# Output products of a SwiGLU block: a 15-product scheme on 2x3 blocks in place of 7-product Strassen, one core of a Trainium2

## The chip, the cores and the metric

The kernel runs on one core of one Trainium2 chip. The metric is the time of one execution on the device in microseconds (us); lower is better. The core has a matrix engine (TensorE, "PE" in the profile, its weight loads "PEld"), a vector engine (VectorE, "DVE"), a scalar engine (ScalarE, "ACT"), GpSimd ("POOL") and a queue engine that here only starts DMA transfers (SyncE, "SP"). Each engine runs its own queue of instructions in order and waits for others through semaphores. SBUF is the on-chip memory of 128 partitions; PSUM is the memory into which PE writes, eight banks of 128 partitions by 512 float32 columns.

## The reference

```python
# x: (8, 4096, 192), weight: (8, 7); w_gate, w_val: (192, 1536); w_out: (1536, 192)
w = softmax(weight, axis=-1)                      # one set of 7 taps for each of 8 heads
out[b, s, h*24 + g] = sum_k w[h, k] * x_pad[b, s + k, h*24 + g]     # 6 zero rows ahead
x = out.reshape(32768, 192)
xn = x / sqrt(mean(x * x, axis=-1) + 1e-6) * rms_g
g = xn @ w_gate
silu = g * (1 / (1 + exp(-g)))
return (silu * (xn @ w_val)) @ w_out              # (32768, 192) float32
```

The weights of the second part come in float64 and are turned to float32 at the start of the kernel. All arithmetic is float32.

## The kernel before

The 32768 tokens are cut into 32 pairs of 1024 (PT). A pair is two groups of 512 tokens (T), held with the 192 features over partitions in three chunks of 64 (KP). The 1536 inner features are 12 chunks of 128 (FC), four units of three (NU, NF).

Pair 0 is computed plainly (plain, L1060, and outer, L1101) while the weights are still being converted. Pairs 1 to 31 use fast matrix products, and each has two stages on PE:

- **Inner products (L798).** For each unit, a scheme of 15 products stands for the 18 plain ones (3 chunks of inner features x 3 chunks of the input x 2 groups). The upper 64 partitions hold the same for the value weights, so each product is two matmuls of 64 rows, which run side by side: half 0 for the gate, half 1 for the value. That is 60 products, 120 matmuls. Between products, ACT and DVE copy, fork and add PSUM banks (Unit.do: S a copy to SBUF, F a bank copied into another, D, C, N and R sums of a bank and a saved tile). G is the SiLU on ACT; M multiplies SiLU and value to a tile of ht, on POOL or DVE (L850).
- **Output products (L938).** The product of the gated tiles with w_out is a Strassen product: 7 products, each over six blocks of 128 inner features (k), in three PSUM banks X, Y and Z. Operands are sums of tiles of the two groups (Pair.sum, L970 and L968: early, nt, more and tls hold them) and differences of blocks of w_out (out_sums, L864, made once in the array x0's place). PE takes them as four column groups of 32 output columns: for a block, two matmuls of 384 token columns on column groups 0 and 1, two of 256 and then two of 128 on groups 2 and 3. Afterwards DVE transposes the results in blocks of 32x32 (turn, L953) and SP stores them (st0, st1, L1024).

Meanwhile the input of a later pair is prepared: DVE does the seven taps in PSUM banks of its own (part_tap, L476, words cv in the order below), ACT the squares (L492), DVE a sum over features, POOL the factor and the scaling (L509, L512, L530); the result goes through DRAM (place) and comes back with tokens along the free axis (fetch_part, tiles xb). Eleven sums of these chunks (XSUM, x_sum, L709 on DVE or POOL; L705 and L706 as a copy and an accumulating DMA) are the other operands of the inner products (xc).

An accumulating DMA (letter Q) is issued from POOL's queue: POOL spends an instruction on it and the addition is done by the transfer, without POOL's arithmetic.

**What sets the order.** ORDER is a list of words, gone through once for each pair. "p2" lets the generator of matmuls (Pair.products) emit two steps. Every other word starts with the engine, V (DVE), A (ACT), G (POOL), Q (accumulating DMA from POOL) or D (DMA queue of SP), and then names a step: "AF0.1.2" is fork 0, half 1, unit 2, on ACT; "GS3.0" is the sum of form 3, block 0, on POOL; "VX3" is entry 3 of XSUM on DVE. A minus at the end means that the step belongs to the pair before. Each engine gets its instructions in the order of its own words; what waits for what is derived from the data. Banks come from two lists of four (free; half 0 and half 1), and a matmul that needs a bank waits for the step that gave it back. In a pair there are 120 steps for inner products, then 84 for output products.

Of the kernel before, what the change touches and what calls it, by code (L numbers as in the profile page):

```python
# [19 lines left out]
def kernel(  # L20
# [68 lines left out]
    SPAN = 1509  # L89
    ORDER = (  # L90
        "p2 GX4- VT11- p2 AS40.0.0 GX9- AS40.1.0 p2 AF0.1.0 AF0.0.0 p2 VC.0.0 Dload- p2",
        "VC.1.0 AS41.0.0 VS41.1.0 p2 AS00.1.0 VS00.0.0 p2 Vbc- VD5.0.0 Gmul- p2 VD5.1.0",
        "AS42.0.0 VS42.1.0 AS51.1.0 p2 AS51.0.0 VR1.0.0 p2 VR1.1.0 VR0.0.0 p2 AF2.0.0 VN.1.0",
        "AG0.0.0 p2 VR0.1.0 AF3.0.0 Dplace- AF3.1.0 p2 GM0.1.0 VR2.0.0 p2 VR2.1.0 AS44.1.0",
        "AS44.0.0 VR5.1.0 p2 AG2.0.0 VR3.0.0 p2 GM2.1.0 AS40.0.1 VR3.1.0 AS40.1.1 p2 VR5.0.0",
        "AG4.0.0 p2 VM4.1.0 AF0.0.1 AG5.0.0 VF0.1.1 p2 AG1.0.0 VS41.0.1 GM5.1.0 p1 AS41.1.1",
        "p1 VC.0.1 AG3.0.0 p1 VC.1.1 p1 GM3.1.0 VS00.0.1 p2 AS42.0.1 VS42.1.1 AS00.1.1 GS3.0",
        "p2 VD5.0.1 p1 VD5.1.1 p1 AS51.0.1 QS1.0 VR1.0.1 AS51.1.1 p2 VR1.1.1 AF2.0.1 GS3.1 p2",
        "AF2.1.1 VR0.0.1 AG1.0.1 p1 VR0.1.1 p1 GM1.1.1 VF3.0.1 AF3.1.1 p2 AG0.0.1 VR2.0.1 p1",
        "VR2.1.1 p1 GM0.1.1 AS44.0.1 AS44.1.1 VR5.0.1 p2 GS2.0 VR5.1.1 p2 AS40.0.2 VR3.1.1",  # L100
        "AS40.1.2 p1 VR3.0.1 GM1.1.0 p1 AG4.0.1 AG3.0.1 p1 VM4.1.1 p1 GM3.1.1 VF0.0.2 AF0.1.2",
        "p2 AS41.0.2 VS41.1.2 p1 AG5.0.1 p1 VC.0.2 GM5.1.1 p1 VC.1.2 p1 AS00.0.2 AS00.1.2 p2",
        "QS1.1 AS42.1.2 AS42.0.2 p2 VD5.0.2 GS3.2 p1 VD5.1.2 p1 AS51.0.2 VR1.0.2 AS51.1.2 p2",
        "GS2.1 VR1.1.2 AF2.0.2 p2 AF2.1.2 VR0.0.2 GS1.2 AG1.0.2 p1 VR0.1.2 p1 AG0.0.2 VF3.0.2",
        "GM1.1.2 p1 AF3.1.2 p1 VR2.0.2 AG2.0.1 p1 VR2.1.2 p1 AS44.0.2 GM2.1.1 AS44.1.2 p2",
        "VR3.0.2 AG2.0.2 GS2.2 p1 VR3.1.2 p1 AS40.0.3 VR5.0.2 AS40.1.3 p2 GM2.1.2 AG4.0.2",
        "VR5.1.2 AG3.0.2 p1 VM4.1.2 p1 AF0.0.3 GM0.1.2 p2 AF0.1.3 VS41.0.3 AS41.1.3 p2",
        "GM3.1.2 AG5.0.2 VC.0.3 p1 VC.1.3 p1 AS00.1.3 GS3.3 AS00.0.3 p2 VS42.0.3 AS42.1.3 p2",
        "GS1.3 VD5.0.3 p1 VD5.1.3 p1 AS51.0.3 GM5.1.2 VR1.0.3 AS51.1.3 p2 VR1.1.3 AF2.0.3 p2",
        "GS2.3 AF2.1.3 VR0.0.3 AG1.0.3 p1 VR0.1.3 p1 GS4.2 VF3.0.3 AF3.1.3 p2 AS44.0.3",  # L110
        "VS44.1.3 p1 GM1.1.3 p1 VR5.1.3 p1 VR5.0.3 p1 Acv0_1 VR3.0.3 AG5.0.3 p1 Vcv1_1 Acv0_2",
        "GM5.1.3 p2 VR3.1.3 AG0.0.3 p2 AG3.0.3 Vcv1_2 DfetA GS3.4 p1 AG4.0.3 p1 VR2.0.3 p2",
        "Acv0_0 Vcv2_2 GM3.1.3 p2 VM4.1.3 p2 Vcv2_1 Ac1 GS3.5 p1 AG2.0.3 p1 Vcv3_1 p2 GS1.4",
        "Vcv3_2 p2 Vcv1_0 p2 GS2.4 p1 Vcv2_0 p2 Vcv4_1 p1 As7 GS1.5 DfetB Dst0- p1 VR2.1.3 p2",
        "Vcv5_1 p1 GM0.1.3 p1 Vcv3_0 p2 Vcv6_1 p1 GS2.5 p1 Vcv4_0 p2 Vcv4_2 GS4.0 p2 Vcv5_0",
        "p2 GS4.1 p1 Vcv6_0 p2 Vcv5_2 Ac2 p1 QX0 p1 Vcv6_2 p2 VM2.1.3 Asq p2 GS4.4 p4 VX3 p1",
        "GS4.3 p4 VX6 p1 QX2 p2 VC22 p2 VX1 p2 GS4.5 VT22 p2 Vred p2 QX8 p3 QX7 p2 VC21 p2",
        "VT21 Gpow p2 VX5 p2 VX10 p2 VT12 p1 Dst1 p1",
# [12 lines left out]
    x0 = cst.tile([P, NJ + HALO, D], F32, name="x0")  # L131
# [328 lines left out]
    def part_tap(p, k, j):  # L460
# [306 lines left out]
    class Unit:  # L767
# [87 lines left out]
    woq = wo_sb[:].rearrange("p (k two) d -> p k two d", two=2)  # L855
    woq = woq.rearrange("p k two (m n e) -> p k two m n e", n=2, e=Q)
    B11, B12, B21, B22 = (woq[:, :, i // 2, :, i % 2, :] for i in range(4))
    NM = D // (2 * Q)
    T1, T2, T3, T4 = (tw[:, i].rearrange("p k (m e) -> p k m e", e=Q) for i in range(4))

    def out_sums():
        for dst, a, b in ((T1, B12, B11), (T2, B22, T1), (T3, B22, B12), (T4, B21, T2)):
            for m in range(NM):
                nc.gpsimd.tensor_tensor(  # L864
                    out=dst[:, :, m], in0=a[:, :, m], in1=b[:, :, m], op=ALU.subtract
                )
                yield
# [450 lines left out]
```

## Time and profile before

| what | value |
|---|---|
| median of 3 runs | 2594.16 us (2594.11 to 2594.45) |
| span of the profiled execution, first to last instruction | 2591.7 us |
| the time up to the first inner product of pair 1 | 125.8 us |
| one pair from 1078.22 us on: inner products, output products | 51.92 us, 27.44 us |
| TensorE clock granted | 1.00 |

"Span" leaves out what lies around the first and last instruction. "Busy" counts time in which an engine executes an instruction. Matmuls overlap: float32 matmuls appear twice in the records, and four column groups work at once, so a mean duration of a matmul is not its cost; the time from one stage's start to the next's is. The same holds more weakly on DVE, where the next instruction starts some 0.08 us ahead of the end of the one before: 512 columns take 0.68 as one instruction and 0.60 from start to start. The last matmul of the run ends at 2586.7 us.

### The profile page before, as it was taken

The numbers are of one execution on the slowest core, as the hardware profiler recorded it, in microseconds if no ns is written. First come the engines' busy times: TensorE is split into PE (matmuls) and PEld (weight loads), VectorE is DVE, ScalarE is ACT, GpSimd is POOL, SyncE is SP. The second block draws the span as 40 slices with busy tenths as digits, with TensorE's granted clock in tenths as the row PEclk, the third lists the DMA queues.
The fourth block names the chain that finished last, engine by engine and source line by source line (L and its number), as shares of the span: only waits on it lengthen the run. The fifth ranks groups of instructions, "written<-read, shape, count | busy, mean of one in ns | idle before, by whom it ended". The sixth has DMA issues, their size and how long they took to land.

```text
span 2591.7 us, 61274 instructions
## 1 busy us (share of the span) xinstructions
PE 2580.3 (100%) x23872; PEld 1777.6 (69%) x23872; DVE 2273.3 (88%) x3681; ACT 1554.2 (60%) x2825; POOL 2078.6 (80%) x1791
## 2 busy tenths in 40 slices
PE   9999999999999999999999999999999999999999
PEld 6876666767667666676666676666766666766666
DVE  8899989888889988889889889898988898898975
ACT  6566555675555765556755557655567555676554
POOL 4887788887778877788877888778888788887777
PEclk9999999999999999999999999999999999999999
DMA  6243554334553335443345433354433455334431
GB/s 145 57 83 59 100 100 87 75 65 90 100 100 77 72 68 104 99 83 77 65 91 100 98 76 69 74 104 96 86 76 66 92 100 94 72 72 80 91 76 22
DMA packets 555887, 216.54 MB, mean 84 GB/s; under 512 B 488782, under 2 KB 491342, under 8 KB 555598
## 3 DMA queue, kind: packets, MB, share of 16 engines
q1 hardware_dynamic: 525644, 164.00, 30.7%
q0 software_dynamic: 26208, 47.72, 10.9%
q8 instruction: 187, 3.06, 0.5%
q10 hardware_dynamic: 3746, 0.92, 0.2%
q14 instruction: 102, 0.84, 0.1%
HBM read 83.84 MB, written 49.55 MB: 51 GB/s over the span
## 4 chain that ended last, share of the span: by engine, by line
PE 98%; DMA 1%; POOL 0%; DVE 0%; issue 0%; SPq 0%; DVEq 0%; POOLq 0%
PE ps L798 62%; PE ps L938 32%; PE ps L1060 2%; PE ps L1101 1%; DMA xb<-xd 0%; POOL tls L970 0%; DMA xc<-xb 0%; DVE xb L647 0%; POOL more L970 0%; SPq L696 0%; DVE wf L338 0%; POOL xc L706 0%; DVE xc L333 0%; DVE o_sb L953 0%; DVE xc L298 0%
## 5 line engine op out<-in xcount | busy, mean ns | idle before, releaser
L798 PE MATMUL ps<-xc,wf 64*128 64x512 f32 x4960 | 1214.6, 591 | 0.0
L798 PEld LDWEIGHTS ps<-xc,wf 64*128 64x128 f32 x4960 | 681.6, 186 | 375.3 <-issue 161.8
L798 PE MATMUL ps<-xb,wf 64*128 64x512 f32 x2480 | 680.3, 591 | 0.0
L747 ACT ACTIVATE tile<-ps 128x512 f32<-128x512 f32 x678 | 391.0, 593 | 388.3 <-PE ps L798 282.7
L747 ACT ACTIVATE tls<-ps 128x512 f32<-128x512 f32 (+1 forms) x562 | 323.5, 588 | 438.9 <-PE ps L798 209.9
L850 POOL TENSOR_TENSOR ht<-ht,tile 128x512 f32<-128x512 f32 x329 | 419.2, 1278 | 125.4 <-ACT tile L843 48.9
L798 PEld LDWEIGHTS ps<-xb,wf 64*128 64x128 f32 x2480 | 354.2, 187 | 182.7 <-issue 91.9
L970 POOL TENSOR_TENSOR early<-ht 128x512 f32<-128x512 f32 x279 | 374.7, 1343 | 42.2 <-DMA ht<-ht 37.3
L850 POOL TENSOR_TENSOR ht<-ht,tls 128x512 f32<-128x512 f32 x260 | 331.2, 1279 | 76.9 <-ACT tls L843 33.2
L747 ACT ACTIVATE ps<-ps 128x512 f32<-128x512 f32 (+1 forms) x589 | 336.1, 581 | 87.6 <-PE ps L938 32.5
L476 DVE SCALAR_TENSOR_TENSOR ps<-xh,tp,ps 128x512 f32<-128x512 f32 x450 | 320.6, 750 | 3.9 <-ACT ps L468 1.7
L938 PE MATMUL ps<-ht,wo_sb 128*32 128x128 f32 (+2 forms) x5208 | 318.3, 380 | 0.0
L938 PEld LDWEIGHTS ps<-ht,wo_sb 128*32 128x32 f32 x5208 | 233.8, 110 | 81.7 <-issue 22.0
L938 PE MATMUL ps<-ht,x 128*32 128x128 f32 (+2 forms) x4464 | 250.7, 379 | 0.0
L830 DVE TENSOR_TENSOR tile<-ps,tile 128x512 f32<-128x512 f32 x349 | 237.8, 684 | 10.2 <-PE ps L798 5.4
L830 DVE TENSOR_TENSOR ht<-ps,tile 128x512 f32<-128x512 f32 x328 | 223.0, 682 | 6.4 <-ACT tile L747 6.4
L938 PEld LDWEIGHTS ps<-ht,x 128*32 128x32 f32 x4464 | 184.4, 110 | 61.2
L843 ACT ACTIVATE tile<-tile 128x512 f32<-128x512 f32 x349 | 214.5, 625 | 0.0
L830 DVE TENSOR_TENSOR ht<-ps,tls 128x512 f32<-128x512 f32 x292 | 199.4, 683 | 6.8 <-ACT tls L747 3.6
L830 DVE TENSOR_TENSOR tls<-ps,tls 128x512 f32<-128x512 f32 x271 | 185.2, 685 | 16.7 <-PE ps L798 13.6
L938 PE MATMUL ps<-early,x 128*32 128x256 f32 (+2 forms) x3348 | 196.0, 379 | 0.0
L938 PEld LDWEIGHTS ps<-early,x 128*32 128x32 f32 x3348 | 143.0, 110 | 44.6
(152 smaller groups left out, 3270.2 us busy)
## 6 DMA issues: line engine op xcount, KB each, us to landing
xb<-xd SPq DMA_DIRECT2D x120, 384.0 KB
xc<-xb SPq DMA_DIRECT2D x120, 256.0 KB
xd<-yn SPq DMA_DIRECT2D x244, 96.0 KB
xh<-in_x_dram SPq DMA_DIRECT2D x192, 105.0 KB
ht<-ht POOLq DMA_DIRECT2D x62, 256.0 KB, 3.3
xc<-xb POOLq DMA_DIRECT2D x60, 256.0 KB, 3.8
xc<-xc POOLq DMA_DIRECT2D x60, 256.0 KB, 4.0
out_dram<-o_sb SPq DMA_DIRECT2D x122, 96.0 KB
```

The costliest lines, as they stand in the source:

```text
L476: nc.vector.scalar_tensor_tensor(out=dst, in0=xk, scalar=w, in1=at, op0=ALU.mult, op1=ALU.add)
L747: nc.scalar.activation(out=dst, in_=src, func=AF.Copy, scale=float(s))
L798: nc.tensor.matmul(out=self.new(v, h, True) if first else self.old(v, h), lhsT=wf[self.u][HALF[h], WAT[i], :], rhs=x_op(XOP[i])[HALF[h]], ...
L830: nc.vector.tensor_tensor(out=self.hv(v) if h else t[:], in0=self.old(v, h), in1=t[:], op=plus(s))
L843: nc.scalar.activation(out=t[:], in_=src[:], func=AF.Silu)
L850: engine[eng].tensor_tensor(out=self.hv(v), in0=src, in1=t[:], op=ALU.mult)
L938: nc.tensor.matmul(out=self.bank(b)[i * Q : (i + 1) * Q, at : at + n], lhsT=left, rhs=cols, start=fresh, stop=True, skip_group_check=True, ...
L970: engine[eng].tensor_tensor(out=dst, in0=a, in1=b, op=op)
L1060: nc.tensor.matmul(out=bank(h, bks[h])[:], lhsT=wf[u][HALF[h], AT[h][k] * NF + f, :], rhs=xb[HALF[h], g, k, :], start=(k == 0), stop=(k == ...
L1101: nc.tensor.matmul(out=bank(h, bks[h])[:, w : w + D], lhsT=hts[f // NF][HALF[h], g, f % NF, j * P : (j + 1) * P], rhs=wo_sb[HALF[h], f, :] ...
```

## The change

Instead of cutting the whole inner dimension for one Strassen product, the output product is done unit by unit: for each of the four units a 2x3 by 3x3 block product (2 groups of tokens, 3 chunks of inner features, 3 blocks of 64 output columns) by 15 products. A product of a unit is one step: four matmuls on the four column groups, each 256 token columns. So there are 60 steps of output products in place of 84. The gated tiles of a unit are called a to f; PLACE says where in ht each lies. OUTS is the order of the 60 products ("11.2" is product 11 of unit 2).

The operands on the token side are eleven sums per unit (SUMS), kept in four registers per unit (AB, CB, X and S) or in a tile itself; several sums overwrite a register whose old value an earlier product reads. Eleven combinations of the w_out blocks are made once by 18 steps on POOL (VSUM), 12 of them where the former 12 stood and six in the course of pair 1. The results gather in five PSUM banks (K, R, N in half 0; C01 and C34 in half 1, each with two results of 256 columns), are forked (FORKS), saved (SNAP) and joined (JOIN) there, and turned by six transposes. Each half pair is stored by four DMAs in place of five.

ORDER is new throughout: it has other engines for some steps of the inner products as well (in words per pair: DVE 108 before and 121 after, ACT 87 and 102, POOL 45 and 45, accumulating DMAs 6 and 12). The tap accumulators of a later pair take one bank of half 0 and two of half 1 instead of two and one.

```diff
     SPAN = 1509
+    PLACE = {'a': 4, 'b': 3, 'c': 5, 'd': 1, 'e': 0, 'f': 2}
+    BANKS = {'K': 0, 'R': 0, 'N': 0, 'C01': 1, 'C34': 1}
+    OUTS = (
+        "11.2 6.2 6.0 4.2 6.3 6.1 11.0 4.1 11.1 4.0 1.0 11.3 1.1 1.2 4.3 9.2 9.0 9.1 8.1 9.3 8.2",
+        "8.0 14.0 5.1 8.3 10.3 5.2 5.0 5.3 13.1 10.0 13.3 7.1 13.0 7.0 14.2 13.2 3.2 7.3 10.2 3.1",
+        "3.3 7.2 14.3 3.0 1.3 14.1 10.1 12.3 2.1 12.1 12.2 12.0 2.2 2.3 2.0 0.3 0.2 0.0 0.1",
+    )
     ORDER = (
...
-        "p2 GS4.1 p1 Vcv6_0 p2 Vcv5_2 Ac2 p1 QX0 p1 Vcv6_2 p2 VM2.1.3 Asq p2 GS4.4 p4 VX3 p1",
-        "GS4.3 p4 VX6 p1 QX2 p2 VC22 p2 VX1 p2 GS4.5 VT22 p2 Vred p2 QX8 p3 QX7 p2 VC21 p2",
-        "VT21 Gpow p2 VX5 p2 VX10 p2 VT12 p1 Dst1 p1",
+        "GX10- Vcv6_1- VD0- Vcv6_2- Asq- p1 AS40.0.0 VD6- VT2- VD2- VT5- p1 VT1- p1 VD3- VT0-",
+        "GX9- VT3- p1 AF0.0.0 VT4- GX8- p3 VC.0.0 AS40.1.0 p1 AF0.1.0 p1 AS41.0.0 VC.1.0 p1 Vred-",
...
+        "p1 VR1.0.2 AG3.0.1 VD5.1.2 GM3.1.1 Gde.0 p2 AS51.0.2 p2 VR1.1.2 p1 AF2.0.2 VR0.0.2",
+        "AS51.1.2 p1 VR0.1.2 p1 Vp4.0 p1 AF2.1.2 AG1.0.2 VR2.0.2 p1 VR2.1.2 p1 AF3.0.2 p1 AF3.1.2",
...
+        "Gcb.1 p1 Gdf.2 VM4.1.2 p2 AF0.1.3 p1 VM0.1.2 VS41.0.3 VC.0.3 VC.1.3 AS41.1.3 AG3.0.2",
+        "VM3.1.2 p2 Vab.2 AS00.0.3 Qde.2 AS00.1.3 p2 GM5.1.2 VD5.0.3 p2 AS42.0.3 VR1.0.3 AS42.1.3",
...
+        "GM0.1.3 VR3.0.3 p2 AS44.1.3 AG2.0.3 VR2.1.3 AG4.0.3 VR3.1.3 GM1.1.3 AG3.0.3 VM2.1.3",
+        "Vdf.3 p2 VM4.1.3 p4 Gp9.2 p1 AS6 Vde.3 p4 GM3.1.3 p1 AG5.0.3 VR5.1.3 VM5.1.3 Gab.3 p1",
+        "Vp4.3 p1 Vp9.0 Gcb.3 Acv0_0 Acv0_1 Gp9.3 p2 AF3 DfetA Vp9.1 Vcv1_1 p1 AF1 Acv0_2 Vcv2_1",
+        "Vcv1_0 p5 AF0 Vcv2_0 p3 Qbe.3 Vcv3_1 Vcv3_0 Gabe.1 p2 Vcv4_0 p2 Qabe.0 Vabe.3 p1 AS8",
+        "Gabe.2 Vbce.1 p3 Qbce.2 AS5 p1 Vcv5_0 Vbce.0 p1 Vcv1_2 Vcv2_2 DfetB p4 Gbce.3 Vcv3_2 p1",
+        "GX3 p1 Vcv4_1 Gbcf.0 Qabd.3 p2 Qabd.2 p1 Dst1- p1 VX6 Vbcf.1 p1 GX0 Vabd.0 AS7 p2 Gbcf.2",
+        "Vabd.1 Vbcf.3 AS13 p1 Vcv6_0 p1 Vcv4_2 p6 VD13 AF4 GX1 Vcv5_1 p5 GX5 AS2 Vcv5_2 GX2 VD1",
+        "VD7",
     )
...
-            if product and v != 5:
+            if product and v != 5 and self.u > 0:
                 i = free[h].pop(0)
...
-    SIDE = (0, 1, 0)
+    SIDE = (0, 1, 1)
+    regs = held + [more[:, i] for i in range(2)]
+    REG = {"AB": 0, "CB": 1, "X": 2, "S": 3}
+    LEFT = {
+        11: ("X", "K"), 9: ("X", "K"), 5: ("CB", "K"), 7: ("CB", "K"), 12: ("CB", "K"),
+        4: ("S", "R"), 8: ("AB", "R"), 13: ("AB", "R"), 2: ("AB", "R"),
+        6: ("e", "N"), 1: ("b", "N"), 3: ("a", "C0"), 10: ("c", "C1"), 14: ("d", "C3"),
+        0: ("f", "C4"),
+    }
+    SUMS = {
+        "ab": ("AB", "a", "b"), "cb": ("CB", "c", "b"), "be": ("b", "b", "e"),
+        "df": ("X", "d", "f"), "de": ("X", "X", "e"), "p4": ("S", "AB", "X"),
+        "p9": ("X", "X", "CB"), "abe": ("AB", "AB", "e"), "abd": ("AB", "AB", "d"),
+        "bce": ("CB", "CB", "e"), "bcf": ("CB", "CB", "f"),
+    }
+    FORKS = {"F3": ("C3", "K", -1), "F1": ("C1", "R", 1), "F0": ("C0", "K", 1), "F4": ("C4", "K", -1)}
+    SNAP = {"S6": "N", "S8": "R", "S5": "K", "S13": "R", "S7": "K", "S2": "R"}
+    JOIN = {
+        "D0": ("C0", "S8", 1), "D1": ("C1", "S5", 1), "D13": ("N", "S13", -1),
+        "D7": ("N", "S7", -1), "D3": ("C3", "S2", -1), "D2": ("K", "S2", 1), "D6": ("K", "S6", -1),
+    }
...
-                for k in range(lo, hi):
-                    src, right = self.left(form, k), RIGHT[form][:, k]
-                    fresh = first and k == 0
-                    two = src.rearrange("p (b q e) -> p q b e", q=2, e=Q)
-                    for i in range(2):
-                        self.tile(b, i, 0, WIDE, right[:, i], src[:, 0:WIDE], fresh)
-                    for i in range(2):
-                        self.tile(b, 2 + i, 0, T // 2, right[:, 2], two[:, i], fresh)
-                    yield
-                    for i in range(2):
-                        self.tile(b, 2 + i, T // 2, T - WIDE, right[:, i], src[:, WIDE:T], False)
-                    yield
+                left = w_out(UNITS[n]) if n in UNITS else right(f"p{n}")
+                cols, to = self.form(src, u), self.part(b)
+                for q in range(NQ):
+                    i, a = divmod(q, 2)
+                    nc.tensor.matmul(
+                        out=to[q * Q : (q + 1) * Q, :], lhsT=left[:, u, a],
+                        rhs=cols[:, i * HALFT : (i + 1) * HALFT], start=fresh, stop=True,
+                        skip_group_check=True, tile_position=(0, q * Q),
+                    )
+                yield
...
+            nc.vector.transpose(out=to[:, n], in_=src.rearrange("p (b e) -> p b e", e=Q))
...
+            engine[eng].tensor_tensor(out=dst, in0=a, in1=b, op=ALU.add)
...
-    later(out_sums(), *[base + 2600 + 60 * i for i in range(4 * NM)])
+    wsum = out_sums()
+    later(wsum, *[base + 2600 + 60 * i for i in range(12)])
...
+                    done_to += 1
+                    if p == 1 and done_to > 30 and done_to % 10 == 0:
+                        next(wsum, None)
```

## The prediction

> **What bounds the kernel now.** I read the page first, then the chain of waits in order of time, then busy time in stretches cut at one pair's two stages, then the groups by form and the timelines of DVE and POOL.
>
> ```profile
> PE 2580.3 (100%) x23872; PEld 1777.6 (69%) x23872; DVE 2273.3 (88%) x3681; ACT 1554.2 (60%) x2825; POOL 2078.6 (80%) x1791
> ...
> PE 98%; DMA 1%; POOL 0%; DVE 0%; issue 0%; SPq 0%; DVEq 0%; POOLq 0%
> ```
>
> PE is never idle: the chain that ended last is 98% PE. The same chain in order of time (start, length, what) shows one pair:
>
> ```profile
> 1078.22 51.93 PE ps L798 x240
> 1130.14 27.44 PE ps L938 x337
> ```
>
> So a pair is 51.92 us of inner products (L798) and 27.44 us of output products (L938), 79.36 together, and 31 pairs run that way. Only shorter PE work can gain, and only while DVE, ACT and POOL keep up. Their work in that pair (stretch, its length, then busy us of PE, PEld, DVE, ACT, POOL):
>
> ```profile
> 1078.22:1157.58 79.36, 79.36 (x746) 54.09 (x746) 68.62 (x113) 48.28 (x87) 62.96 (x52) 1.00 0.41 82
> 1078.22:1130.14 51.92, 51.92 (x244) 33.07 (x248) 45.61 (x75) 41.68 (x77) 39.98 (x32) 1.00 0.30 49
> 1130.14:1157.58 27.44, 27.44 (x507) 21.02 (x506) 23.02 (x39) 6.60 (x11) 22.98 (x21) 1.00 0.62 145
> ```
>
> DVE has 10.7 us to spare per pair, POOL 16.4. In the waits, PE's loads do wait for others, but at most 0.7 us at a time, inside the running matmul:
>
> ```profile
> PEld ps L798 <- ACT ps L747: 46.2, 126, 0.7
> ```
>
> The last view is DVE beside POOL, because the change adds sums to both. Two DVE lines and two POOL lines of one moment (start, length), then the groups:
>
> ```profile
> 828.85 3.38 DVE L709 TENSOR_TENSOR xc<-xb,xc 128x512 f32<-128x512 f32 x1
> 832.48 0.56 DVE L991 TENSOR_TENSOR tls<-ps,tls 128x384 f32<-128x384 f32 x1 [0.25 <-PE ps L938]
> ```
>
> ```profile
> 828.86 1.57 POOL L970 TENSOR_TENSOR tls<-ht,nt 128x512 f32<-128x512 f32 x1
> 830.11 1.56 POOL L970 TENSOR_TENSOR more<-ht,nt 128x512 f32<-128x512 f32 x1
> ```
>
> ```profile
> L709 DVE TENSOR_TENSOR xc<-xb,xc 128x512 f32<-128x512 f32 x65 | 92.6, 1425 | 14.2 <-DMA xc<-xb 12.6 <-DMA xb<-xd 0.2
> L706 POOL DMA_DIRECT2D xc<-xc x60 | 64.3, 1071 | 27.1 <-DMA xc<-xb 23.8 <-issue 1.2 <-DVE tls L991 0.9
> L709 DVE TENSOR_TENSOR xc<-xc 128x512 f32<-128x512 f32 x62 | 44.7, 721 | 1.2 <-DMA xc<-xc 0.2
> L709 DVE TENSOR_TENSOR xc<-xb 128x512 f32<-128x512 f32 x34 | 27.4, 808 | 0.4 <-DMA xb<-xd 0.4
> L968 POOL DMA_DIRECT2D ht<-ht x62 | 56.1, 905 | 10.0 <-POOL early L970 10.0
> ```
>
> A DVE add of two SBUF operands takes 0.69 us where POOL is quiet. At 828.85 it took 3.38: it ended 0.56 after POOL's second sum. DVE reads one operand from PSUM in nearly all its other work and is not held.
>
> **PE's part.** Removed per pair: 7 products x 6 blocks = 42, each 384 columns on two column groups beside 256+128 on the other two, 27.44/42 = 0.6533 us. Added: 15 products x 4 units = 60, each 256 columns on all four groups. By columns, 0.6533 x 256/384 = 0.4355, x60 = 26.13: 1.31 saved. Lower bound of the new stage by L798's rate (51.92/60 = 0.8653 for 512 columns): 0.4327 x 60 = 25.96, 1.48 saved. Upper bound by a straight line through both points (0.8653 at 512, 0.6533 at 384, so 0.0173 fixed per product): 0.4413 x 60 = 26.48, 0.96 saved. I take 1.31, the row of the same kind of tile. Loads stay in step: 12 per 0.6533 before, 8 per 0.4355 after. 31 x 1.31 = 40.6 us (29.8 to 45.9). New pair: 78.05 us.
>
> **DVE.** I count the new ORDER word by word, with start-to-start distances in this timeline: 0.60 for 512 columns, 0.47 for 384, so about 0.34 for 256 (estimate from these two); a 256 transpose about 0.38 (the pair 256+128 takes 0.65). From 68.62 come off: 8 copies (S 10 to 5, F 5 to 2) 4.8, the two L991 joins 1.0, four turns of 256+128 2.5, four x sums 2.7. On go: 7 joins of 256 columns 2.4, 6 transposes 2.3, 4 more gate products of two SBUF operands 2.4, 14 block sums at 0.62 8.7. Sum 73.4 of 78.05: 4.6 to spare, before any wait for POOL. Adds of two SBUF operands go from 6 to 20 per pair.
>
> **ACT.** 48.28, plus 3 F and 5 S at 0.49, plus ten copies of 256 columns at 0.37, less three of 384 at 0.48: 54.5. It hides under PE's 78.05; without that cover it is 6.2 per pair.
>
> **POOL.** 43 full sums and gate products before (19+22+2) and after (15+20+8), so no difference there. DMA sums go from 6 to 12: 6 x 0.87 (the unhindered issue; the means are 0.91 and 1.07) = 5.2, so 68.2 of 78.05. Behind each such issue the next sum waits in POOL's queue, and the sum lands 3.3 to 4.0 later by the issue rows.
>
> **SP.** Four stores for five per half pair and two x copies for four; fetch, mark and load keep their turn. The second store moves behind the fetches; its issue needs only PE's and DVE's old results. Nothing behind it (x copies, load) is needed within 10 us. Zero, at the price of 2 us per pair if a store held the transposes of the next pair back.
>
> **The start and the end.** 18 weight sums for 12 on POOL, of 256 columns for 192: 0.6 to 0.8 each, so 11 to 14 us for 7. Six are spread in pair 1, whose output stage is 52 us later. Zero, at most 7 once. At the end 6 transposes stand for 4 turns, and both stores are late: before, 5.0 us lie between the last matmul and the end; I take the same, plus or minus 2.
>
> **The new wait.** The stretch of the output stage up to the sum Gbcf.2, which product 12.2, the 52nd, reads: 51 x 0.4355 = 22.2 us after the stage's start. POOL's queue there holds 12 sums (1.23 each in the timeline) = 14.8 and 5 DMA issues = 4.4. The first sum overwrites what product 11.2 reads, so it starts at 0.44 at best. DVE has 11 two-SBUF adds in the stretch, 6.7 us, in which POOL's sums can't run if they exclude each other as at 828.85. Those adds can lie beside the 4.4 of issues at best: 0.44+14.8+4.4+2.3 = 21.9, no stall. If none does, 26.3, a stall of 4.1. So 0 to 4.1 per pair. I take a ninth, 0.45: DVE's 31 gate products L850 with two SBUF operands took 0.69 each, so an order can put such work between POOL's sums, and both engines wait for the same products here, so some exclusion falls into waits that exist anyway. 31 x 0.45 = 14.
>
> The Trainium skill, "SBUF — State Buffer", section "Who interferes with whom", says the same of such an add against a GpSimd instruction that reads SBUF: who starts first keeps the port for the whole instruction, the other blocks. The trace agrees (3.38 for 0.69) and shows more, since the add sat out two POOL sums. By the page's one instruction, an add at a random moment would wait half of 1.23 in 56 of 78 us: 0.44 each, 8.8 per pair, DVE at 82.2, and the time 2594 + 31 x 2.8 = 2681; this speaks against the change.
>
> **The sum.** The profiled execution has a span of 2591.7; the median is 2594.2, 2.5 more, which lies outside the instructions and stays. 2594.2 - 40.6 + 14 = 2567.6, so 2568. Its own range: 2551 (saving 45.9, stall near 0, end 2 later) to 2588 (saving 40.6, stall 1.1 per pair). About 0.2%, 5 us, is what a measurement can tell from no change.
>
> **The rivals.**
>
> Slower: the shared port makes DVE the bound. Place: all 20 two-SBUF adds, seven of them placed among the inner products, where the kernel before has none and PE's loads have at most 0.7 us in hand. Price: before, L709's DVE rows sum to 164.7 us in 30 pairs, 5.5 each, for 5 adds of 0.69: 0.41 of waiting per add. 20 x 0.41 = 8.2, DVE 81.6 per pair, 2594 + 31 x (81.6 - 79.36) = 2664. It decides from (79.36-73.4)/20 = 0.30 per add. For it: the 0.41, and POOL busy 68 of 78. Against: L850's rows, and that the new order leaves DVE 5 us short of full in the output stage (its words there sum to 20.8 of 26.1) and gives 12 sums to DMA. Chance 0.36.
>
> No change: late DMA sums or POOL's stall eat the gain. 12 DMA sums landing in 3.3 to 4.0 were costed at issue alone; Qbce.2 is placed 11 products (4.8 us) ahead of its reader and needs 0.9 + 4.0 = 4.9. A stall of 1.3 per pair leaves 2594. Chance 0.06.
>
> The products don't get shorter: with 256 columns every product pays what 384 paid, 60 x 0.6533 = 39.2, +11.8 per pair, 2959. Against: the loads per us are the same as before. Chance 0.02.
>
> PE alone decides, no stall, and the rate of L798 holds: 2594.2 - 45.9 = 2548. Chance 0.03, just outside.
>
> **How the numbers follow.** Forecast 0.53, port 0.36, no change 0.06, long products 0.02, best 0.03. Faster: 0.53 + 0.03 = 0.56; same 0.06; slower 0.38. The port's price runs from 0.30 per add (2594) through 0.38 (about 2640) to more; half of it lies under 2640. The range 2550 to 2640 leaves out the best case's 0.03, long products' 0.02 and some 0.15 of the port's.
>
> **What would show it.** In the chain, a pair of 51.9 and 26.1 (25.96 to 26.48) confirms the products; more than 0.5 of idle on PE per pair, released by POOL or DVE sums around product 52, is the wait that I priced. Rows of DVE adds with a mean over 0.99 (0.69 + 0.30), DVE busy over 78 and PE idle in the inner products show the port. DVE at 72 to 77 per pair, POOL at 67 to 72 and ACT at 53 to 56 confirm the counts. Wrong altogether would be a PE product of more than 0.4413, or PE waiting for a DMA.

## The result and the profile after

The changed kernel took 3085.38 us (median of 4 runs, 3080.45 to 3088.46), and the kernel before 2594.30 beside it (4 runs, 2594.11 to 2594.82). The ratio is 1.1892 (95% interval 1.1875 to 1.1909): slower by 491 us, where 2568 was forecast and 2640 was the top of the range.

The page of the changed kernel, span, busy time of the engines and chain of waits:

```profile
span 3086.6 us, 61417 instructions
...
PE 2708.5 (88%) x23128; PEld 1604.5 (52%) x23128; DVE 2869.7 (93%) x3964; ACT 1745.6 (57%) x3290; POOL 2393.7 (78%) x1979
...
PE 55%; DVE 31%; issue 7%; ACT 3%; DMA 2%; POOL 0%; DVEq 0%; ACTq 0%; POOLq 0%
```

PE is no longer what bounds the kernel throughout. It holds 55% of the chain, where it held 98%, and DVE holds 31%, where it held nothing. DVE's busy time rose by 596 us. One pair in stretches (whole, inner products, output products; then its length, busy us of PE, PEld, DVE, ACT and POOL, granted clock, DMA share and GB/s):

```profile
1182.50:1278.27 95.77, 83.78 (x724) 48.55 (x721) 90.03 (x124) 54.25 (x103) 75.06 (x60) 0.95 0.42 81
1182.50:1237.06 54.56, 53.94 (x244) 32.41 (x240) 50.12 (x80) 46.59 (x88) 42.04 (x35) 1.00 0.35 59
1237.06:1278.27 41.21, 29.84 (x481) 16.14 (x481) 39.91 (x46) 7.66 (x16) 33.02 (x25) 0.88 0.52 110
```

The inner products went from 51.92 to 54.56 us and the output products from 27.44 to 41.21. In the output stage DVE is busy for 39.91 of 41.21 us, and PE for 29.84. Over all pairs, from the starts of the matmuls: the inner stage grew by 2.90 us in the mean (51.96 to 54.86, 31 stages) and the output stage by 13.37 (27.45 to 40.82, the 30 that an inner stage follows). 31 x 2.90 + 30 x 13.37 = 491, so the two stages hold the whole difference.

The groups by form (out<-in, shape, count, busy us and mean ns of one, idle time ahead of them):

```profile
L1000 DVE TENSOR_TENSOR early<-early,ht 128x512 f32<-128x512 f32 x217 | 309.5, 1472 | 7.6 <-PE ps L979 7.6
L713 DVE TENSOR_TENSOR xc<-xb,xc 128x512 f32<-128x512 f32 x35 | 138.5, 3959 | 1.2 <-POOL xc L713 1.2
L854 DVE TENSOR_TENSOR ht<-ht,tile 128x512 f32<-128x512 f32 x92 | 130.2, 1416 | 1.6
L854 DVE TENSOR_TENSOR ht<-ps,tile 128x512 f32<-128x512 f32 x78 | 53.5, 686 | 4.7 <-ACT tile L847 1.3 <-PE ps L802 1.2
L979 PE MATMUL ps<-early,wo_sb 128*32 128x256 f32 x2232 | 204.2, 535 | 268.1 <-DVE early L1000 268.1
```

The third and fourth rows are the same instruction on DVE, a gate product of 512 columns, with one difference: the third reads both operands from SBUF and takes 1.416 us in the mean, the fourth reads one from PSUM (ps) and takes 0.686. All 619 adds and products of two SBUF operands on DVE after pair 0 have a mean of 1.492 us, 0.80 above the 0.69 of an unhindered one; 20 of them per pair make 16 us. Before, 181 such adds lost 0.30 each. The last row shows where PE pays: it was idle for 268.1 us ahead of products whose sum `early` came from DVE. The waits (who waited for whom: us in total, times, longest):

```profile
PE ps L979 <- DVE early L1000: 269.5, 64, 8.9
PEld ps L802 <- ACT tile L751: 84.1, 153, 1.4
PE ps L979 <- DMA early<-ht: 17.2, 24, 1.9
```

Before, PE's loads waited at most 0.7 us for another engine (ACT). Now one wait for a DVE sum lasts up to 8.9. The chain in order of time (start, length, what) shows that wait in the pair above:

```profile
1258.11 2.63 DVE xc L713
1260.74 2.76 issue
1263.50 6.76 DVE early L1000 x4
1270.39 7.95 PE ps L979 x96
```

96 records, eight for each product, are the last 12 of the 60: PE stood before product 12.3, the 49th, which reads Vbcf.3. What held that sum is seen in the timelines (start, length, instruction). DVE, then POOL:

```profile
1258.02 5.55 DVE L713 TENSOR_TENSOR xc<-xb,xc 128x512 f32<-128x512 f32 x1
1263.50 6.75 DVE L1000 TENSOR_TENSOR early<-early,ht 128x512 f32<-128x512 f32 x4
```

```profile
1257.53 1.74 POOL L998 DMA_DIRECT2D early<-ht  x2
1258.68 1.90 POOL L713 TENSOR_TENSOR xc<-xb 128x512 f32<-128x512 f32 x1
1259.92 1.88 POOL L1000 TENSOR_TENSOR early<-early,ht 128x512 f32<-128x512 f32 x1
1261.16 1.86 POOL L713 TENSOR_TENSOR xc<-xb,xc 128x512 f32<-128x512 f32 x1
1263.09 1.60 POOL L713 TENSOR_TENSOR xc<-xc 128x512 f32<-128x512 f32 x1
1264.65 1.71 POOL L713 TENSOR_TENSOR xc<-xb,xc 128x512 f32<-128x512 f32 x1
```

DVE's x sum 6 (VX6) starts at 1258.02, while POOL issues two DMA sums (Qabd.3, Qabd.2), and ends at 1263.57. In that time POOL does three sums without a gap, 1.24 us from start to start, the last ending at 1263.02. The DVE add ends 0.55 after it: it sat out all three. The four block sums behind it then alternate with POOL's x sums, at 1.69 us each. So 5 adds, which take 0.69 each alone, hold DVE from 1258.02 to 1270.25, and Vbcf.3 is the last of them.

PE pays a second time. Its own timeline, before the wait, after it, and after that:

```profile
1240.11 0.61 PE L979 MATMUL ps<-nt,wo_sb 128*32 128x256 f32 x8
1240.54 0.61 PE L979 MATMUL ps<-more,x 128*32 128x256 f32 x8
...
1270.39 6.22 PE L979 MATMUL ps<-early,wo_sb 128*32 128x256 f32 x64 [8.88 <-DVE early L1000]
1276.42 1.92 PE L979 MATMUL ps<-ht,x 128*32 128x256 f32 x32
```

An unhindered product takes 0.43 us from start to start (1240.11 to 1240.54). The 8 products behind the wait took 6.03 (1270.39 to 1276.42), not 8 x 0.4355 = 3.48. Stretches of 2 us show why; the eighth column (after the length, the five engines) is the granted clock:

```profile
1263.00:1265.00 2.00, 0.00 (x0) 0.00 (x0) 2.00 (x2) 0.00 (x0) 1.92 (x3) 1.00 0.00 0
1267.00:1269.00 2.00, 0.00 (x0) 0.00 (x0) 2.00 (x2) 0.00 (x0) 2.00 (x2) 0.50 0.00 0
1271.00:1273.00 2.00, 2.00 (x28) 0.99 (x23) 2.00 (x4) 0.00 (x0) 2.00 (x3) 0.50 0.20 35
1275.00:1277.00 2.00, 2.00 (x36) 1.25 (x32) 1.21 (x3) 0.64 (x3) 0.00 (x0) 0.84 0.39 66
```

PE went idle at 1261.5. The clock fell to 0.50 3.9 us later, and came back 5.2 us after PE had resumed. The mean clock of the whole run is 0.950; before, it was 1.00.

### The profile page after: what moved, and what is told of

Its sections match the earlier page's. It is cut to its first block, busy times and chain, and to the rows that moved or that the text cites. A ratio compares the mean times of both kernels' runs of the same rounds, so it can differ in the third digit from the quotient of the medians.

```text
span 3086.6 us, 61417 instructions
## 1 busy us (share of the span) xinstructions
PE 2708.5 (88%) x23128; PEld 1604.5 (52%) x23128; DVE 2869.7 (93%) x3964; ACT 1745.6 (57%) x3290; POOL 2393.7 (78%) x1979
## 4 chain that ended last, share of the span: by engine, by line
PE 55%; DVE 31%; issue 7%; ACT 3%; DMA 2%; POOL 0%; DVEq 0%; ACTq 0%; POOLq 0%
PE ps L802 44%; DVE early L1000 11%; PE ps L979 8%; DVE ps L480 7%; DVE ht L854 4%; DVE xc L713 2%; PE ps L1080 2%; DMA xb<-xd 2%; DVE more L1000 2%; PE ps L1121 1%; DVE nt L1000 1%; DVE ps L818 1%; DVE tls L1000 1%; ACT tls L847 1%; ACT ps L751 1%
## 5 line engine op out<-in xcount | busy, mean ns | idle before, releaser
L802 PE MATMUL ps<-xc,wf 64*128 64x512 f32 x4960 | 1490.5, 598 | 23.6 <-ACT tile L751 15.4
L802 PE MATMUL ps<-xb,wf 64*128 64x512 f32 x2480 | 926.5, 592 | 0.0
L751 ACT ACTIVATE tile<-ps 128x512 f32<-128x512 f32 (+1 forms) x853 | 475.3, 573 | 324.6 <-PE ps L979 210.4
L979 PE MATMUL ps<-early,wo_sb 128*32 128x256 f32 x2232 | 204.2, 535 | 268.1 <-DVE early L1000 268.1
L979 PE MATMUL ps<-ht,x 128*32 128x256 f32 x5952 | 390.4, 380 | 0.0
L854 POOL TENSOR_TENSOR ht<-ht,tile 128x512 f32<-128x512 f32 x232 | 318.2, 1378 | 72.5 <-ACT tile L847 67.9
L854 POOL TENSOR_TENSOR ht<-ht,tls 128x512 f32<-128x512 f32 x233 | 320.0, 1380 | 63.2 <-ACT tls L847 57.4
L1000 DVE TENSOR_TENSOR early<-early,ht 128x512 f32<-128x512 f32 x217 | 309.5, 1472 | 7.6 <-PE ps L979 7.6
L1000 POOL TENSOR_TENSOR early<-early,ht 128x512 f32<-128x512 f32 x186 | 279.8, 1504 | 37.0 <-PE ps L979 36.8
L979 PE MATMUL ps<-early,x 128*32 128x256 f32 x4216 | 286.0, 380 | 19.0 <-DMA early<-ht 17.2
L979 PEld LDWEIGHTS ps<-early,wo_sb 128*32 128x32 f32 x2232 | 99.7, 152 | 372.5 <-issue 330.3
```

What stands on the lines that cost most here:

```text
L751: nc.scalar.activation(out=dst, in_=src, func=AF.Copy, scale=float(s))
L802: nc.tensor.matmul(out=self.new(v, h, True) if first else self.old(v, h), lhsT=wf[self.u][HALF[h], WAT[i], :], rhs=x_op(XOP[i])[HALF[h]], ...
L854: engine[eng].tensor_tensor(out=self.hv(v), in0=src, in1=t[:], op=ALU.mult)
L979: nc.tensor.matmul(out=to[q * Q : (q + 1) * Q, :], lhsT=left[:, u, a], rhs=cols[:, i * HALFT : (i + 1) * HALFT], start=fresh, stop=True, s ...
L1000: engine[eng].tensor_tensor(out=dst, in0=a, in1=b, op=ALU.add)
```

## The experiments

All times are compared with the kernel before on the same chip, whose median was 2593 to 2595 us in every group of runs. Stage lengths are medians from the starts of the matmuls, unless called a mean: the inner stage (51.92 before, 54.58 after) and the output stage (27.44 before, 41.04 after). In this section all kernels but e12 were timed once. Unless a diff shows otherwise, the kernel is the changed one. My theory after the result was that DVE's second SBUF operand and POOL's sums exclude each other; the rivals were the late DMA sums, the number of sums itself, and the product scheme.

### Is it the second operand in SBUF?

e1_one_operand lets DVE's 20 two-operand SBUF instructions (block sums, x sum 6, gate products) read one operand and leave the other out, in an instruction of the same 512 columns. The kernel then no longer computes the reference. The edit at the block sums, the other two likewise:

```diff
+            if eng == "V":
+                nc.vector.tensor_reduce(
+                    out=dst, in_=b.rearrange("p (t o) -> p t o", o=1), axis=AX.X, op=ALU.add
+                )
+                return
             engine[eng].tensor_tensor(out=dst, in0=a, in1=b, op=ALU.add)
```

> All 20 DVE instructions per pair that read two SBUF operands (14 block sums, x sum 6, five gate products) read one operand instead, as a reduction over one element: the second operand is left out. Port theory (DVE's second SBUF read and POOL's sums exclude each other): these rows fall to about 0.6 to 0.7 us each, POOL's sums back to 1.28, PE idle under 1.5 us per pair, time 2555 to 2640. Rival (DVE is simply too full, or its order comes too late, whatever POOL does): the rows change little in number and length of work, PE keeps waiting, time above 2900.

Measured: 2668.46. The number of sums, their places and POOL's work are what they were, and 417 of the 491 us are gone. The instructions take 0.68 us each. With the operand goes the wait for it, but that is small: in the changed kernel DVE was idle for 17 us in all ahead of these instructions. The inner stage is 52.47, the output stage 28.7 (mean 29.35), and the granted clock 0.99. The rival over 2900 falls. My own range ended at 2640, 28 short: what is left was something else. The waits of this kernel, then a stretch of its chain:

```profile
PEld ps L991 <- DMA early<-ht: 84.0, 34, 4.0
...
PE ps L991 <- DMA early<-ht: 68.3, 30, 3.5
```

```profile
1091.35 0.24 issue
1091.59 6.24 DMA early<-ht
1097.88 11.86 PE ps L991 x216
```

PE waits for a DMA sum that lands 6.24 us after its issue, where I had costed 3.3 to 4.0. In those 6.30 us the DMA engines were busy with other transfers as well: the share is 1.12, against 0.57 in the 10 us ahead of it. That these transfers are what delays it is not shown.

```profile
1091.60:1097.90 6.30, 4.43 (x87) 2.40 (x80) 6.19 (x10) 0.77 (x2) 5.55 (x5) 1.00 1.12 245
```

e8_one_operand_abe_pool takes e1 and turns the one DMA sum that the chain names into a POOL sum:

```diff
-        "Vcv1_0 p5 AF0 Vcv2_0 p3 Qbe.3 Vcv3_1 Vcv3_0 Gabe.1 p2 Vcv4_0 p2 Qabe.0 Vabe.3 p1 AS8",
+        "Vcv1_0 p5 AF0 Vcv2_0 p3 Qbe.3 Vcv3_1 Vcv3_0 Gabe.1 p2 Vcv4_0 p2 Gabe.0 Vabe.3 p1 AS8",
```

> On top of the kernel in which 20 DVE instructions read one operand only (the second is left out), the DMA sum abe.0 becomes a POOL sum. Late-transfer theory (with the port out of the way, what is left is the 6 to 7 us that this DMA sum takes while the input fetches fill the DMA engines): PE's waits for that transfer vanish, 1.3 to 2.5 us per pair, time 2590 to 2630. Rival (POOL's queue is late itself and the transfer only comes last): PE waits for POOL instead, time 2650 or more.

Measured: 2582.26, 8 under the range expected. PE's waits for DMA shrink to this:

```profile
PEld ps L991 <- DMA early<-ht: 11.1, 21, 1.7
...
PE ps L991 <- DMA early<-ht: 3.8, 6, 1.2
```

That run reached its first inner product at 131.8 us, where the others are at 124 to 126. e12_again is the same kernel once more, in three rounds, to see whether that start belongs to it.

> The kernel with one operand in 20 DVE instructions (the second left out) and abe.0 on POOL once more, timed against the kernel before in rounds: in the one look at it the inner products of pair 1 began at 131.8 us instead of 125, in a part that is the same in all these kernels. If that was chance, 2574 to 2577 and a ratio of 0.992 to 0.994; if it belongs to this kernel, 2581 to 2584.

Measured: 2579.73 (2578.89 to 2584.19, 4 runs) against 2594.78 (7 runs), ratio 0.9948 (0.9931 to 0.9965). The start was at 124.9, so it had been chance; the time lies between the two expectations. One of its pairs in stretches, as above:

```profile
1306.82:1385.60 78.78, 78.78 (x722) 49.01 (x722) 73.72 (x124) 53.91 (x103) 69.64 (x61) 1.00 0.50 96
1306.82:1359.56 52.74, 52.74 (x244) 33.51 (x248) 48.10 (x81) 46.36 (x88) 45.07 (x40) 1.00 0.44 74
1359.56:1385.60 26.04, 26.04 (x482) 15.50 (x482) 25.62 (x44) 7.54 (x16) 24.57 (x21) 1.00 0.61 139
```

This is the changed kernel without the exclusion and without the late DMA sum. In this pair PE is never idle, DVE works 73.72 us, and the output stage is 26.04.

e5_no_sums leaves the block sums out from pair 2 on:

```diff
+            if self.p > 1:
+                return
```

> From pair 2 on all 44 block sums per pair are left out (on DVE, POOL and by DMA); the products read what the registers hold. If the 60 products cost what was worked out, 26.0 to 26.5 us of output products per pair and 51.9 of inner products, time 2548 to 2575. If the products themselves or the forks, joins and transposes hold PE, the stage stays above 28 us and the time above 2620.

Measured: 2587.76, with an output stage of 26.04 and an inner stage of 52.47. So the products are shorter as planned (27.44 to 26.04), and the scheme itself isn't what costs time. My expectation was missed by 13 us on the upper side. Pair 1, which still has its sums, has stages of 57.14 and 41.21, some 20 us over those of the later pairs; without that the time would lie within the range. The inner stage is 0.55 over that of the kernel before even with no sums in it. The trace shows small waits of PE's loads spread over the new order there; I did not track them down.

### Two engines alone, one operand against two

e6_port is a kernel of its own: stretches of eight DVE instructions of 512 columns beside eight POOL instructions, in four of which POOL first issues an accumulating DMA.

```python
nc.vector.tensor_tensor(out=vc[:], in0=va[:], in1=vb[:], op=ALU.add)     # two in SBUF
nc.vector.tensor_tensor(out=vc[:], in0=bank[:], in1=vb[:], op=ALU.add)   # bank in PSUM
nc.gpsimd.tensor_tensor(out=pc[:], in0=pa[:], in1=pb[:], op=ALU.add)
nc.gpsimd.dma_start(out=qa[:], in_=qb[:], accum_op=ALU.add)
```

> A kernel of its own, which computes nothing of the reference: eight DVE instructions of 512 columns beside eight of POOL, in seven phases. Port theory: DVE alone 0.6 to 0.7 us per two-SBUF add; POOL alone 1.24 per sum; both at once DVE's adds take 1.2 to 1.9 each, in turn with POOL's sums; behind a DMA issue on POOL the DVE adds wait for several POOL sums in a row (over 3 us); with one operand in PSUM, or with one operand at all, 0.6 to 0.7 throughout. Rival (no exclusion, only a slower memory): all two-SBUF adds get slower by the same factor, and so do those with one SBUF operand.

Measured: 0.69 us for a DVE add alone and 1.26 for a POOL sum alone. Together they go strictly in turn: DVE 1.63, POOL 1.59, one of each every 1.665. With one operand in PSUM, or with one operand only, DVE stays at 0.69 while POOL works. Behind an issue one add took 2.1 to 2.6, and the next ones 1.63. The hold of over 3 us that I expected there did not come. In this kernel each POOL sum overwrites the tile of the one before, which leaves gaps of 0.08 us between them.

e7_port_free changes that: POOL's sums write eight tiles, so they follow each other without a gap. (Each stretch also starts with a few small copies more, and one has the issue in second place.)

```diff
-    def pool():
-        nc.gpsimd.tensor_tensor(out=pc[:], in0=pa[:], in1=pb[:], op=ALU.add)
+    def pool(i=None):
+        to = pc if i is None else pd[i]
+        nc.gpsimd.tensor_tensor(out=to[:], in0=pa[:], in1=pb[:], op=ALU.add)
```

> Computes nothing of the reference: as the first kernel of this kind, but POOL's sums write eight different tiles, so that none waits for another. If POOL sums that follow each other without a gap keep the port, DVE's adds wait for several of them (over 3 us); if only those behind a DMA issue do, the phases with an issue show one DVE add of over 3 us and the phase without one shows adds of 1.6 us in turn. Rival (always in turn): 1.6 us everywhere, 2.6 at most behind an issue.

The DVE timeline of this kernel. From the top: eight adds with one POOL sum beside the first two, eight beside POOL's sums, eight behind an issue with the sums after it, and eight behind an issue with one operand in PSUM. POOL's side of the third stretch follows:

```profile
18.83 6.71 DVE L30 TENSOR_TENSOR vc<-va,vb 128x512 f32<-128x512 f32 x8
...
42.53 13.33 DVE L30 TENSOR_TENSOR vc<-va,vb 128x512 f32<-128x512 f32 x8
...
60.23 15.96 DVE L30 TENSOR_TENSOR vc<-va,vb 128x512 f32<-128x512 f32 x8
...
115.46 5.76 DVE L33 TENSOR_TENSOR vc<-bank,vb 128x512 f32<-128x512 f32 x8
```

```profile
60.49 1.00 POOL L45 DMA_DIRECT2D qa<-qb  x1 [0.37 <-issue]
61.23 8.83 POOL L42 TENSOR_TENSOR pd<-pa,pb 128x512 f32<-128x512 f32 x7
69.77 1.50 POOL L42 TENSOR_TENSOR pc<-pa,pb 128x512 f32<-128x512 f32 x1
```

Without an issue the adds take turns (13.33 for 8, 1.66 each). Behind one, the first add passes, the second starts at 60.95 and ends 10.88 us later, 0.56 after the last of POOL's eight sums, and the rest take 0.69. Another issue in the middle, or the issue in second place, gave holds of 10.16 and 9.34. The hold at 1258.02 looks the same, and in these two kernels it takes both, an issue ahead and a run of sums without a gap.

The traces of both full kernels say the same. I sorted their two-operand SBUF adds by how many POOL sums they sat out. Those that sat out two to four sums (3.3 to 5.6 us), 14 before and 33 after, all stand beside a run of POOL that follows an issue without a gap. Of some 300 that met POOL with no issue ahead, none sat out more than one. An issue ahead isn't enough by itself: over 200 adds of the changed kernel that have one in the run sat out a single sum. Before, the 14 long holds made 41 of the 53 us that the two-operand adds lost; after, the 33 make 156 of 496. What in the issue makes POOL keep its place stays open.

### One add, two DMA sums, all DMA sums

e2_x6_pool moves the add that is held (VX6) to POOL.

```diff
-        "... p1 VX6 Vbcf.1 p1 GX0 ..."
+        "... p1 GX6 Vbcf.1 p1 GX0 ..."
```

> x sum 6 is done by POOL in its place of the order instead of by DVE. Port theory: the hold of 5.5 us in front of it is gone, the four block sums behind it start earlier, PE's idle of 8.9 us per pair shrinks by 3 to 6: time 2900 to 2990. Rival (DVE too full): DVE loses one add of 0.6 us per pair, time 3060 or more.

Measured: 3070.71, where the port theory expected at most 2990 and the rival 3060 or more. The hold moved on to the next add in DVE's queue, Vbcf.1, which took up to 6.91 us, and 33 adds still sat out three or four sums. It is not that add; it is whichever stands there. The time fits the rival, yet the hold is there as before: the expectation had named the victim, not the cause.

e3_abd_pool takes away the issues instead: the two DMA sums become POOL sums.

```diff
-        "GX3 p1 Vcv4_1 Gbcf.0 Qabd.3 p2 Qabd.2 p1 Dst1- ..."
+        "GX3 p1 Vcv4_1 Gbcf.0 Gabd.3 p2 Gabd.2 p1 Dst1- ..."
```

> The two DMA sums abd.3 and abd.2, which stand in POOL's queue just ahead of the x sums, become POOL sums. Run-behind-an-issue theory (a DMA issue lets POOL's next sums run without a gap, so a DVE add behind it waits for three or four of them, 5.5 us at x sum 6): no DVE add waits for more than one or two POOL sums at that place, its 5.5 us fall to 1.7 to 2.5, PE's idle of 8.9 us shrinks by 2 to 4, time 2950 to 3030. Rival (POOL's queue is simply full there): the holds of 5 us stay, POOL has 0.7 us more, time 3080 to 3110.

Measured: 2959.79, as expected, with more work on POOL (2423.9 us busy, 2393.7 before the edit). The x sum 6 that took 5.55 now takes 1.35 in the median, and at most 1.75 (that source line's durations: minimum, median and maximum in ns, then the first and last start):

```profile
L713 DVE TENSOR_TENSOR xc<-xb,xc x35: 676/1351/1752, 117.6 to 2850.4; 128x512 f32<-128x512 f32 x35
```

PE's wait for DVE's early sums falls from 269.5 to 150.8 us, the clock rises to 0.971, and the output stage shrinks to 36.68.

e9_no_dma_sums makes POOL sums of all ten Q block sums.

```diff
-        "... Qde.1 p1 Qbe.0 ... Qde.2 ... Qbe.2 ... Qbe.1 ... Qbe.3 ... Qabe.0 ... Qbce.2 ... Qabd.3 p2 Qabd.2 ..."
+        "... Gde.1 p1 Gbe.0 ... Gde.2 ... Gbe.2 ... Gbe.1 ... Gbe.3 ... Gabe.0 ... Gbce.2 ... Gabd.3 p2 Gabd.2 ..."
```

> All ten DMA sums per pair (be, de, abe, bce, abd) become POOL sums in their places; two DMA x sums stay. If the runs behind DMA issues and the late transfers are what the kernel with abd.3 and abd.2 on POOL (2960 us) still loses besides the adds that go in turn with POOL's sums, no DVE add waits over 2.5 us, PE never waits for a DMA, and the time is 2820 to 2920, although POOL has 10 x 0.37 = 3.7 us more per pair. If POOL's queue in the output stage is the bound instead, 2960 to 3080.

Measured: 2986.01, within the range named for the other case. No add takes longer than 1.81 us any more and PE waits for no DMA sum, yet 552 of 619 adds sit out one sum: POOL has more sums, so more adds meet one. The mean is 1.39, and the loss per add 0.70 in place of 0.80. Long holds are a part of the loss, and the plain turns, one sum for one add, are the larger one.

e11_no_dma_sums_act adds to e9 that seven copies per pair (VS and VF) go from DVE to ACT, to give DVE room.

```diff
-        "... VS44.0.0 ... VF0.1.1 ... VF3.0.1 ... VS41.0.2 ... VS42.0.2 ... VS41.0.3 ... VS44.0.3 ..."
+        "... AS44.0.0 ... AF0.1.1 ... AF3.0.1 ... AS41.0.2 ... AS42.0.2 ... AS41.0.3 ... AS44.0.3 ..."
```

> On top of the kernel without DMA sums, seven copies and forks of the inner products per pair go from DVE to ACT: 4.2 us less for DVE, 3.5 more for ACT (54 of some 90). If DVE with its held adds is the engine that everything waits for, 60 to 130 us faster than the kernel without DMA sums; if POOL is, no change within 20.

Measured: 3088.48, which is 102 over e9 and misses both expectations. PE's loads of the inner products wait longer for ACT, to which the copies have moved. e9, then e11, in the waits:

```profile
PEld ps L802 <- ACT tile L751: 69.7, 158, 1.1
```

```profile
PEld ps L802 <- ACT tile L751: 127.9, 254, 1.6
```

ACT is 60% busy there. The inner stage grows by 1.73 in the mean, some 54 us in all. The output stage grows by 1.58 (37.07 to 38.65), and what does that was not traced. Spare time on an engine doesn't make a place in its queue free at the right moment.

### Which of the two stages, and can POOL take the sums?

e10_inner_one_operand lets only the seven adds that lie among the inner products read one operand and leaves the other out: block sums p4.0, ab.2 and df.3 and four gate products. The edit at the sums, the gate products likewise:

```diff
+            if eng == "V" and (name, u) in (("p4", 0), ("ab", 2), ("df", 3)):
+                nc.vector.tensor_reduce(
+                    out=dst, in_=b.rearrange("p (t o) -> p t o", o=1), axis=AX.X, op=ALU.add
+                )
+                return
```

> Of the 20 DVE instructions with two SBUF operands only the seven placed among the inner products read one operand (the second is left out): sums p4.0, ab.2, df.3 and four gate products. Port theory: inner products fall from 54.58 to 52.5 us per pair (that is the part of the 2.7 us lost there which the holds of these adds make up); the output stage changes by under 2 us; time 2960 to 3030. Rival (the inner products are late because of the new order of ACT's and DVE's words): 54.2 us or more remain, time over 3050.

Measured: 2934.42, 26 under the range expected. The inner stage falls from 54.58 to 52.47, as in e1, so these seven adds cost it 2.1 us. The output stage gains too, by 2.7 (mean 38.14 for 40.82) where under 2 was expected. Perhaps DVE enters it with less left to do; that was not traced.

e4_sums_pool moves DVE's 14 block sums and the x sum to POOL:

```diff
-        "Vdf.3 p2 VM4.1.3 p4 Gp9.2 p1 AS6 Vde.3 ...", "Vp4.3 p1 Vp9.0 ... Vp9.1 ...",
-        "... Vabe.3 ...", "... Vbce.1 ... Vbce.0 ...", "... VX6 Vbcf.1 p1 GX0 Vabd.0 ...", "Vabd.1 Vbcf.3 ...",
+        "Gdf.3 p2 VM4.1.3 p4 Gp9.2 p1 AS6 Gde.3 ...", "Gp4.3 p1 Gp9.0 ... Gp9.1 ...",
+        "... Gabe.3 ...", "... Gbce.1 ... Gbce.0 ...", "... GX6 Gbcf.1 p1 GX0 Gabd.0 ...", "Gabd.1 Gbcf.3 ...",
```

(p4.0 and ab.2 among the inner products likewise.)

> The 14 block sums and x sum 6 that DVE does go to POOL, each in its place of the order. Port theory: DVE has only its five gate products left to wait with, but POOL's work is 68.2 + 15 x 1.24 = 86.8 us per pair and becomes the bound: 2594 + 31 x (86.8 - 79.4) = 2825, up to 2950 with waits, so faster than 3085 although 9 us of work were moved to an engine that needs twice as long for it. Rival (the exclusion costs little and order or data set the time): POOL's 18.6 us more come on top, time above 3200.

Measured: 3334.28, slower than the changed kernel, nearly 400 over the range of the port theory and within the rival's. DVE is 65% busy and POOL 84%, and the output stage is 47.8. The waits of this kernel:

```profile
PEld ps L979 <- POOL early L1000: 348.8, 124, 8.2
...
PE ps L979 <- POOL early L1000: 287.1, 112, 7.8
```

My estimate had been POOL's load over a whole pair. But 13 of the 15 moved sums crowd into the output stage or right ahead of it, where their readers are, and POOL does them at half DVE's speed (1.26 us against 0.69 in e6). By its time alone the run fits the rival, and it doesn't decide about the port: it has few two-operand adds left (156, 1.04 each). It shows that moving the sums to POOL in their places costs more than it frees.

## Why the prediction was wrong, step by step

**The products: right.** I took a saving of 1.31 us per pair, with bounds 0.96 and 1.48. With the sums out of the way a stage takes 26.04, against 26.13 predicted, and saves 1.40.

**The counts of work: right.** In e12, where nothing waits for the port, DVE works 73.7 us in a pair (73.4 predicted) and ACT 53.9 (54.5). POOL works 69.6; with a sum in place of an issue, 68.2 + 1.23 - 0.87 = 68.6 follows from the prediction. In the changed kernel itself ACT has 54.25, but DVE 90.03 and POOL 75.06, since time in which an instruction is held counts as busy.

**The start and the end: right.** The first matmul of the inner products starts at 125.0 in both kernels (the table of the kernel before has 125.8). From the last matmul to the end of the span it is 6.8 us, 5.0 before, within my 2. SP's stores hold nobody in the waits.

**"The new wait" is the step that failed:** "So 0 to 4.1 per pair. I take a ninth, 0.45". The place was right: PE stands before product 49, and I had named the stretch up to the 52nd. The price was not: PE waits 269.5 / 31 = 8.7 us per pair for DVE's early sums, over twice my upper bound. With the waits for other sums and the lower clock behind them the output stage took 40.82 in the mean, where 26.13 + 0.45 had been forecast. Three things in that step were wrong.
- I asked how late POOL's queue would be. The late engine was DVE. I had let DVE's adds lie "beside the 4.4 of issues" as the best place for them, where POOL does no arithmetic; the runs show that beside an issue, with a run of sums behind it, is the worst place, for there an add was held until POOL's whole run was over (5.55 us in the pair shown, 10.88 in e7).
- My reason for the low end, L850's 31 rows of 0.69, showed that one order had found a quiet place for one add. In the new one the gate products of two SBUF operands, L854, take 1.21 in the mean. A row of an unhindered instruction says where POOL was then, not where it will be.
- I had shown that an add of 0.69 took 3.38 when POOL ran, and then raised the number of such adds from 6 to 20 while treating the wait as something that an order could avoid. The row ahead of the two POOL rows that I showed for that moment is an issue, and the prediction made no use of it:

```profile
828.26 0.87 POOL L706 DMA_DIRECT2D xc<-xb  x1 [1.42 <-DMA xc<-xb]
```

**The port rival was right in kind and too small.** It took 0.41 of waiting per add from the kernel before. Even that was misread: the three rows hold 161 adds and not 150, so 164.7 / 161 - 0.69 = 0.33, and by this the rival's own sum would have given some 2616 in place of 2664. The changed kernel has 0.80: some 425 of its 619 adds sat out a POOL sum or more, against 36 of some 180 before. By its own sum 20 x 0.80 = 16.1 gives a DVE of 89.5 and 2594 + 31 x (89.5 - 79.36) = 2908; the measured DVE is 90.0. The other 177 us are what the rival's form left out: a pair is 95.8 long for 90.0 of DVE. DVE and PE now wait for each other in turn, and the clock falls in PE's waits; how the 177 divide between the two was not measured. If the 2.55 us of the pair shown are lost in all 30, that is 76 us (an estimate; the mean clock of 0.950 fits half speed for some 10 us in every pair).

**How the 491 us come about,** with the port taken away first (taken away in another order, the parts would come out otherwise):

| part | us | from |
|---|---|---|
| DVE's second SBUF operand against POOL's sums, with the clock that falls in the waits | 417 | after less e1 |
| the DMA sum abe.0 that lands late | 89 | e1 less e12 |
| shorter products | -42 | (27.45 - 26.04) x 30 |
| inner products in the new order | 16 | (52.49 - 51.96) x 31, e12 |
| rest of the output stage | 11 | (26.40 - 26.04) x 30, e12 |

The parts of the first line by stage are 2.35 x 31 = 73 in the inner products and 11.47 x 30 = 344 in the output products.

**Late DMA sums: right in kind.** The "no change" rival had named them, with bce.2 as the one and 4.0 us as the landing time. It was abe.0, with over 6 in e1. In the changed kernel this is mostly hidden (PE waits 17.2 us in all for such sums, its loads 30.9), since DVE is later still; it shows only once the port is out of the way.

**Not in the sum at all** was a longer inner stage. I had left it at 51.92, and only the port rival named it. It grew by 2.90 in the mean: 2.35 go with the second operand (e1), and 0.55 remain with no port and no sums. The rival by which the products don't get shorter falls.

**The rule of the Trainium skill.** The Trainium skill, "SBUF — State Buffer", section "Who interferes with whom", has a DVE instruction of two SBUF inputs and a GpSimd instruction that reads SBUF exclude each other, one whole instruction at a time. The trace agrees with its kind: 1.63 for two SBUF operands beside POOL, 0.69 for one or for one in PSUM. It goes beyond it in length: the 10.88 of e7 and the 5.55 of the changed kernel are runs of POOL's instructions. The 2681 that I had worked out beside that rule was still 400 short.

**A faster version.** None was found. The fastest of the changed kernels that leave nothing out is e3, at 2959.79. e12, which leaves operands out, shows what these products give in this order if every one of its adds meets a quiet POOL: 0.5% under the kernel before. With the 16 and 11 us of the table gone as well it would be some 2552 (an estimate: 2594 - 42). No order was made with the exclusion counted.

## What to carry to other kernels

Before giving an engine more instructions of a kind that the profile shows held even a few times, count how many the change adds, and price each at the held row, not the quiet one; then ask what an order built without that cost will do to it. Test such a suspicion by letting the instruction read one operand: the number, place and length of the work stay, and what goes besides the exclusion is the wait for the other operand, which the idle time ahead of those rows bounds. An engine's mean load over a pair says little about a stage into which its work crowds, as e4 and e11 showed.

## What was unexpected of the hardware

**Behind an accumulating DMA issued by POOL, turns can become a run.** DVE adds with two SBUF operands and POOL sums otherwise alternate: 1.63 to 1.66 us for an add of 0.69, and 1.59 to 1.70 for a sum of 1.26. Behind an issue, with sums that follow each other without a gap, one add waits for all of them: 10.88 us for the sums of e7. With gaps of 0.08 us between the sums it was 2.1 to 2.6.

**A wait of PE costs more than its length.** PE was idle for 8.9 us; the granted clock fell to 0.50 3.9 us into it and came back 5.2 us after PE had resumed, so 8 products took 6.03 us and not 3.48. The Trainium skill, "TensorE: Matmul & The Clock Gate", Part 1, has the clock at half after at least one idle window of about 3.4 us and whole again after at least one busy window as long. The trace agrees with both.
